# Attention and gated convolution in one kernel: the written order is planned anew, with a new model of the DMA queue

## The chip, the cores and the metric

The kernel runs on one core of a Trainium2 chip. The metric is the device time of one execution in microseconds (us), lower is better. Before the change it is 386.22 us (median of 3 runs, 385.4 to 386.39).

## What is computed

For each of 8 batches and 12 heads, with 448 rows and 64 columns a head, in float32:

```python
scores = q @ k.T / 8
m = scores.max(-1)
e = exp(scores - m)
attn = e / (e.sum(-1) + exp(-m) + 1e-9)       # softmax with one more in the sum
x = attn @ v                                   # heads side by side: 448 x 768 a batch
x1, x2, x3 = split(x @ w_proj, 3)              # w_proj is 768 x 2304
c = irfft(rfft(x2, axis=rows) * rfft(filter))  # circular convolution along the 448 rows
out = (x1 * c * x3) @ w_out
```

## The kernel before, in words

Matmuls run in bfloat16. Two heads form a pair: six pairs a batch, 48 in all, numbered 0 to 47. For pair i the kernel has these steps, named by the tokens that they make in the code:

- Loads of q, k and v (192 or 224 KB each), cast to bfloat16 by GpSimd (POOL). For the first two batches (`staged`, pairs 0 to 11) TensorE (PE) transposes q and k, step `T`. For the others (`loaded`) a DMA does it, a "turn" (`k_turn`, `q_turn`, tokens `kT` and `qT`): one pair each for batch 2, three pairs each from batch 3 on.
- `S(i,0..3)`: four groups of scores on PE (lines 772 and 774). ScalarE (ACT) takes the exponential of each (lines 785 and 791). `ER` and `V(i,0..1)`: the products with v (lines 803 and 811). `norm` on VectorE (DVE, lines 824 to 826) divides and leaves `xb`.
- `X`: xb transposed into xT, by PE in batch 0 and by a DMA of three pairs (`x_dma`, line 896) after that.

Then, a batch b at a time, the dense part (`dense`):

- `fold` and `xf` on DVE (lines 954 to 962): sums and differences of xT, two halves of three pairs.
- `P(b,pg,ch)`: eight groups of six matmuls for x2 (line 985). `Z`: 8 matmuls into the spectrum (line 1012), copied by ACT (`xs`, line 1020), multiplied and added by DVE (`t` and `yh`, lines 1026 and 1032).
- `I(b,0..5)`: the way back (line 1097), copied by ACT (line 1106), put together by DVE (`cw`, `cv`, `y`, lines 1115 to 1141).
- `G(b,0..5,0..1)`: twelve groups of six for x1 and x3 (line 1058), drained by ACT (line 1070) and DVE (line 1073).
- `O`: the groups for the output (line 1170), drained by ACT (line 1182) and stored.

The filter's spectrum (`hps`, lines 724 and 727, 16 matmuls) is made once. The weights come in pieces through POOL's queue, cast on the way: `LOADS` names them, (1,0) and (1,1) the two halves for P, (0) and (2) for G, "F" the filter, "O" w_out (`wout`, line 755).

No engine chooses its order at run time. `Plan` holds all steps as tasks, each with an engine, a cost, a due time ("want"), the tokens that it needs and makes, and for a DMA the time that it takes on the transfer engines. `Plan.run` walks through planned time, and when an engine is free it takes the first task within a window of 160 that is ready, in order of due times. The outcome is one fixed sequence of instructions for each engine; semaphores hold them to the data. So a wrong cost makes no wrong result, but it may put an instruction too early in a queue, and all that stands behind it on that queue waits with it. SyncE's queue (SP) issues all loads, turns and stores in such a sequence. The due times come from tables: `ATT` and `SLOT` (attention), `DENSE` and `PACE` (dense part), `FOLD`, `LEAD` (how long before its pair a load, cast or turn is due), `LOAD` (weights). In the first 36 us of planned time gaps on PE are filled with matmuls of zeros (line 1256), behind 38 at the start (line 1264).

Planned costs before the change, and one of the lines that hold them:

```python
    LANDING = 2.2
    LEAD = [4.72, 83.18, 8.95, -3.90, 7.63, -20.62, 94.14]
    add("SP", 1.3, tau(g) - LEAD[6], lambda hp=hp: q_turn(hp), need=[("cq", i) for i in gs] + [last],
        make=[("qT", i) for i in gs], dma=0.5 * few, late=0.7)
```

Of the kernel before, what the change touches and what calls it, by code (L numbers as in the profile page):

```python
# [20 lines left out]
SP = 112  # L21
# [20 lines left out]
class Plan:  # L42
# [10 lines left out]
    LAT = {"PE": 0.2, "ACT": 0.22, "DVE": 0.2, "POOL": 0.15, "SP": 0.0}  # L53
    LANDING = 2.2
    OPEN = 8
# [12 lines left out]

    def add(self, eng, cost, want, emit, need=(), make=(), take=(), give=(), dma=0.0, run=256, n=1, after=0.0, begun=(), late=0.0):
        self.tasks.append((want, len(self.tasks), eng, cost, emit, need, make, take, give, dma, after, run, n, begun, late))  # L70

    def run(self):
# [13 lines left out]
        gone = {}  # L86
        free = {e: self.BEGIN for e in queue}
        now, order = 0.0, []
        events = [0.0] + sorted({t[10] for t in self.tasks})
        queues = {"SP": [], "POOL": []}  # L90
# [166 lines left out]
def kernel(  # L257
# [124 lines left out]
    def staged(b):  # L382
# [3 lines left out]
        for hp in range(NHP):  # L386
# [5 lines left out]
            for n, (name, x, at, size) in enumerate(parts):  # L392
                src = stage(g, at, size)

                def load(name=name, x=x, src=src, hp=hp, g=g):
# [12 lines left out]
                first = name == "q" and g == 0  # L408
                add("ACT" if first else "SP", 0.52, -21.0 if first else want + 0.1 * n, load, need=need,
                    make=[("s" + name, g)], dma=0.75 if name == "q" else 0.7 if g or name == "v" else 1.5, run=1024 if name == "q" else 768,  # L410
                    begun=[("i" + name, g)])
                if hp == 0 and name != "q":
                    add("SP", 0.5, want + (0.05 if name == "k" else SLOT[0] + 0.05) if b == 0 else want - RE1 + 0.1 * n,
                        lambda name=name, x=x: nc.sync.dma_start(rests[:, "kv".index(name)], shared(x, b)),
                        need=[("cr" + name, b - 1)] if b else (), make=[("r" + name, b)],
                        dma=1.05, begun=[("ir", b)])

# [107 lines left out]
    def loaded(b):  # L525

        i0 = b * NHP
        few = 1 if b == NSTAGED else 3
# [17 lines left out]
        for n, (name, x) in enumerate((("k", k), ("v", v))):  # L546
            add("SP", 0.5, tau(i0) - LEAD[0] - 0.2 + 0.1 * n,
                lambda name=name, x=x: nc.sync.dma_start(rests[:, "kv".index(name)], shared(x, b)),
                need=[("cr" + name, b - 1)], make=[("r" + name, b)], dma=1.05)
        for u in range(2):  # L550
            c = slice(64 * u, 64 * u + 64)
            add("POOL", 0.6, tau(i0) - LEAD[1] - 0.2, lambda c=c: nc.gpsimd.tensor_copy(kn[c, :, 0, c], rests[c, 0]),
                need=[("rk", b)] + (["zero kn"] if b == NSTAGED else [("kT", i) for i in range(i0 - NHP, i0)]), make=[("crk", b)])
        add("POOL", 0.56, tau(i0) - LEAD[3], lambda: nc.gpsimd.tensor_copy(vn[b % 2][:, :, 3, 0:DH], rests[:, 1]),
            need=[("rv", b), ("V", i0 - NHP - 1, 1)], make=[("crv", b), ("vr", b)])

        for hp in range(NHP):
            g = i0 + hp
            n = g - NHP * NSTAGED
            qsrc = qrooms[n % QS]  # L560
            add("SP", 0.52, tau(g) - LEAD[4],
                lambda hp=hp, qsrc=qsrc: nc.sync.dma_start(
                    qsrc.rearrange("p (u c) -> p u c", u=2),
                    q[b, 2 * hp : 2 * hp + 2].rearrange("u (p j) d -> p u (j d)", j=NST),
                ),
                need=[("cq", g - QS)] if n >= QS else staged_done, make=[("sq", g)], dma=0.75, run=1024)
            add("POOL", 0.65, tau(g) - LEAD[5],
                lambda hp=hp, qsrc=qsrc: nc.gpsimd.tensor_copy(  # L568
# [4 lines left out]
            if hp % few == 0:  # L573
                gs = range(g, g + few)
                add("SP", 1.3, tau(g) - LEAD[6], lambda hp=hp: q_turn(hp), need=[("cq", i) for i in gs] + [last],
                    make=[("qT", i) for i in gs], dma=0.5 * few, late=0.7)
            for n, (name, x) in enumerate((("k", k), ("v", v))):
# [4 lines left out]
                    ("T", i) for i in range(NHP * NSTAGED - NHP, NHP * NSTAGED)]  # L582
                add("SP", 0.52, tau(g) - LEAD[0] + 0.1 * n,
                    lambda x=x, hp=hp, src=src: nc.sync.dma_start(src.rearrange("p (u c) -> p u c", u=2), rows(x, b, hp)),
                    need=room, make=[("s" + name, g)], dma=0.7, run=768)
                sv = src.rearrange("p (u j d) -> p u j d", u=2, j=3)
                if name == "k":
                    add("POOL", 0.6, tau(g) - LEAD[1],
                        lambda hp=hp, sv=sv: nc.gpsimd.tensor_copy(
# [170 lines left out]
    def attention(i):  # L760
# [168 lines left out]
    def dense(b):  # L929
# [264 lines left out]
        def O(st, ch):  # L1194
# [42 lines left out]
    with (  # L1237
# [102 lines left out]
```

## Time and profile before

| what | value |
|---|---|
| median of 3 runs | 386.22 us |
| span of the profiled execution | 384.4 us |
| what lies around the span: median less span | 1.8 us |
| PE busy | 364.9 us, 95% |
| PE loading weights | 232.4 us, 60% |
| DVE busy | 261.8 us, 68% |
| ACT busy | 264.1 us, 69% |
| POOL busy | 112.2 us, 29% |
| DMA packets, bytes | 116333, 64.43 MB |

The profile is of one execution. Its time as a run is not given beside it, so its own time is its span and 1.8 us around it, as the median has it. PE's busy time counts the matmuls of zeros too. A wait is put down to what ended it last. The share of DMA is the mean over 16 DMA engines, and it can pass 1 where packets overlap.

### The profile page before, as it was taken

Reading aid. Unit: us, or ns where it says so; the run is one execution under the profiler, and the core shown is the slowest. Engines: PE = TensorE matmul, PEld = TensorE weight load, DVE = VectorE, ACT = ScalarE, POOL = GpSimd, SP = SyncE. Lnnn points to the kernel's source line nnn. Section 1 sums busy time; section 2 is a strip of 40 time slices with the busy share of each in tenths; the row PEclk is TensorE's granted clock in tenths of the full one; section 3 lists DMA queues with packets and bytes.
Section 4 is the critical chain, followed back from the end, with each engine's and each line's share of the span. In section 5 each row is a group of like instructions: output and inputs, shape, how many; then the busy total and the mean of one; then the engine's idle time right before and its main releaser. Section 6 shows DMA issues by size and latency. Waiting matters only on the chain.

```text
span 384.4 us, 9536 instructions
## 1 busy us (share of the span) xinstructions
PE 364.9 (95%) x3700; PEld 232.4 (60%) x3700; DVE 261.8 (68%) x667; ACT 264.1 (69%) x460; POOL 112.2 (29%) x240
## 2 busy tenths in 40 slices
PE   7887799999998999889989999999999999999995
PEld 6555575557654676545755666565665567667553
DVE  6575758996868357997596576665488725987660
ACT  5698487884885868767756658886778587444543
POOL 5692436141835533445552411110000000000000
PEclk9999999999999999999999999999999999999999
DMA  8999998599999999999999933592302132200214
GB/s 207 265 225 232 249 219 197 131 178 218 262 269 273 249 261 244 263 230 251 247 241 226 274 112 100 102 210 96 84 3 43 41 124 43 43 1 2 82 41 165
DMA packets 116333, 64.43 MB, mean 168 GB/s; under 512 B 73085, under 2 KB 112704, under 8 KB 116288
## 3 DMA queue, kind: packets, MB, share of 16 engines
q1 hardware_dynamic: 111568, 58.18, 63.5%
q0 software_dynamic: 4480, 5.41, 8.3%
q8 instruction: 29, 0.48, 0.5%
q10 hardware_dynamic: 240, 0.23, 0.3%
q14 instruction: 16, 0.13, 0.1%
HBM read 43.86 MB, written 11.01 MB: 143 GB/s over the span
## 4 chain that ended last, share of the span: by engine, by line
PE 65%; DVE 13%; DMA 12%; ACT 4%; issue 2%; POOL 2%; SPq 2%; POOLq 0%; DVEq 0%; ACTq 0%
PE psum L1058 19%; PE psum L985 14%; PE psum L1170 12%; PE psum L811 6%; PE psum L772 5%; DMA nat<-in_k_dram 5%; DMA xT<-xb 3%; DVE t L1026 2%; DMA nat<-in_v_dram 2%; PE psum L1097 2%; PE psum L1012 2%; DMA nat<-in_q_dram 2%; DVE xf L962 2%; DVE yh L1032 2%; ACT e L785 2%
## 5 line engine op out<-in xcount | busy, mean ns | idle before, releaser
L785 ACT ACTIVATE e<-psum 128x896 bf16<-128x896 f32 x144 | 126.4, 925 | 21.8 <-PE psum L772 21.6
L1058 PE MATMUL psum<-xT,wproj_bf 128*128 128x448 bf16 x576 | 122.4, 352 | 0.1
L1058 PEld LDWEIGHTS <-wproj_bf 128*128 128x128 bf16 x576 | 53.5, 97 | 42.8 <-issue 1.3
L985 PE MATMUL psum<-wproj_bf,xf 128*113 128x384 bf16 x384 | 69.1, 326 | 1.5 <-DVE g L1073 0.7
L985 PEld LDWEIGHTS <-xf 128*113 128x113 bf16 x384 | 50.0, 132 | 15.3 <-issue 3.4
L1170 PE MATMUL psum<-wout_bf,yT 128*128 128x384 bf16 x288 | 52.9, 326 | 0.0
L811 PE MATMUL psum<-vn,e 128*128 128x65 bf16 x1152 | 44.7, 194 | 0.0
L1070 ACT CAST x<-psum 128x448 bf16<-128x448 f32 x48 | 25.6, 534 | 25.8 <-PE psum L1058 24.5
L1026 DVE TENSOR_TENSOR t<-xs,hrs 113x768 bf16<-113x768 bf16 (+1 forms) x64 | 37.0, 613 | 8.0 <-ACT xs L1020 8.0
L772 PE MATMUL psum<-qT,kT 64*128 64x448 bf16 x288 | 40.8, 355 | 0.6 <-ACT kT L485 0.4
L1182 ACT COPY osb<-psum 128x384 f32<-128x384 f32 x56 | 26.4, 484 | 21.3 <-PE psum L1170 20.0
L811 PEld LDWEIGHTS <-e 128*128 128x128 bf16 x1152 | 39.2, 97 | 2.8
L568 POOL CAST nat<-nat 112x512 bf16<-112x512 f32 x36 | 24.1, 671 | 52.6 <-DMA nat<-in_q_dram 49.2
L1170 PEld LDWEIGHTS <-yT 128*128 128x128 bf16 x288 | 27.5, 98 | 19.2 <-issue 1.5
L824 DVE TENSOR_SCALAR rec<-psum 128x8 f32<-128x8 f32 x48 | 7.7, 161 | 44.8 <-PE psum L811 44.3
L1073 DVE TENSOR_TENSOR g<-x,psum 128x448 bf16<-128x448 bf16 x48 | 29.5, 615 | 11.9 <-PE psum L1058 9.5
L999 ACT CAST x<-psum 113x384 bf16<-113x384 f32 x32 | 15.5, 483 | 28.7 <-PE psum L985 28.5
L826 DVE TENSOR_TENSOR xb<-psum,rec 128x512 bf16<-128x512 f32 x48 | 33.2, 691 | 1.7
L1020 ACT CAST xs<-psum 113x384 bf16<-113x384 f32 (+1 forms) x64 | 28.2, 499 | 3.8 <-PE psum L1012 3.6
L1106 ACT CAST cr<-psum 128x452 bf16<-128x452 f32 x48 | 25.3, 547 | 7.0 <-PE psum L1097 6.6
L791 ACT ACTIVATE er<-psum 128x448 bf16<-128x448 f32 x48 | 26.7, 556 | 4.6 <-PE psum L774 4.6
L997 DVE CAST x<-psum 113x384 bf16<-113x384 f32 x32 | 17.5, 550 | 14.1 <-PE psum L985 14.1
(111 smaller groups left out, 435.7 us busy)
## 6 DMA issues: line engine op xcount, KB each, us to landing
nat<-in_q_dram SPq DMA_DIRECT2D x47, 224.0 KB, 4.7
out_dram<-osb SPq DMA_DIRECT2D x24, 384.0 KB, 2.4
nat<-in_k_dram SPq DMA_DIRECT2D x41, 192.0 KB, 4.9
nat<-in_v_dram SPq DMA_DIRECT2D x41, 192.0 KB, 4.9
wproj_bf<-in_moe_w_proj_dram POOLq DMA_DIRECT2D x2, 1152.0 KB, 17.3
rests<-in_k_dram SPq DMA_DIRECT2D x8, 192.0 KB, 4.9
rests<-in_v_dram SPq DMA_DIRECT2D x8, 192.0 KB, 5.2
out_dram<-osb SPq DMA_DIRECT2D x8, 192.0 KB, 2.9
```

The costliest lines, as they stand in the source:

```text
L772: nc.tensor.matmul(sc[:, u, 0:S], kT[b % 2][c, hp, t, :], qT[b % 2][c, hp, :])
L785: nc.scalar.activation(to, of, AF.Exp, scale=SCALE)
L791: nc.scalar.activation(to, of, AF.Exp, scale=SCALE)
L811: nc.tensor.matmul(out_bank(u)[:, n, :], P["e"][1 + t][:, u * S + n * 128 : u * S + n * 128 + 128], vn[b % 2][:, hp, 4 * u + t, :], start= ...
L826: nc.vector.tensor_tensor(W["xb", b][:, hp].rearrange("p n (u d) -> p u n d", u=2), op[:, :, :, 0:DH], rec[:].unsqueeze(3).to_broadcast([1 ...
L985: nc.tensor.matmul(pps[:FQ, :DCH], W["xf", b][:, pg, kt, 0:FQ], wproj_bf[:, kt, D + ch * DCH : D + (ch + 1) * DCH], start=(kt == 0), stop= ...
L1020: nc.scalar.copy(L["xs", par, ch][:K, pg % 2, :], L["Z", pg, ch][:K, :DCH])
L1026: nc.vector.tensor_tensor(t[:K], L["xs", par, ch][:K], h, op=ALU.mult)
L1058: nc.tensor.matmul(p[:, :S], wproj_bf[:, kt, 2 * part * D + dt * 128 : 2 * part * D + (dt + 1) * 128], xT()[:, kt, 0:S], start=(kt == 0), ...
L1073: nc.vector.tensor_tensor(g[:, dt, :], L["x1", dt], p[:, :S], op=ALU.mult)
L1170: nc.tensor.matmul(ops[:n, :DCH], y[:, dt, 0:n], wout_bf[:, dt, ch * DCH : (ch + 1) * DCH], start=(dt == 0), stop=(dt == NDT - 1),)
L1182: nc.scalar.copy(L["os", st][:n, ch * DCH : (ch + 1) * DCH], L["O", st, ch][:n, :DCH])
```

## The change

It changes no computation and no instruction: every engine has the same instructions (but for the matmuls of zeros, 76 at line 1256's place in the code where there were 97). It changes what the planner believes, and so the order and the places of the instructions on every queue.

- A DMA that transposes (`turn=True`) now holds the planned SP queue: SP is free again 0.7 before the transfer ends or 0.86 after the issue began, whichever is later. Before, SP was free after 1.3.
- The planned duration of each transfer is new, as is the landing (1.95 for 2.2), and an issue costs SP 0.3 for 0.5.
- `LEAD` is a table per batch, where one row served all.
- All due times are new. Among what follows from them: through POOL's queue the weights go as F, (1,0), (0), (1,1), (2), O, where it was (1,1), (0), F, (1,0), (2), O; w_out is issued behind the casts of pair 13, where it was behind those of pair 16; the filter's spectrum stands ahead of the first P; O of batch 0 and of batch 2 stand soon after their I, where they stood 17 and 36 us of PE work behind.

```diff
-    LANDING = 2.2
+    LANDING = 1.95
+    TURN_ISSUE, TURN_LEAD = 0.86, 0.7
+    SHIFT = {}
...
+                        if h[2][15]:
+                            free[e] = max(clock - self.TURN_LEAD, begin[h[2][1]] + self.TURN_ISSUE)
+                            heapq.heappush(events, free[e])
                         done(h[2], clock + self.LANDING + h[2][14], "SP")
...
-                    q.append([end, t[9], t])
+                    if t[15]:
+
+                        begin[t[1]], free[e] = now, 1e9
+                    q.append([now + 0.3 if t[15] else end, t[9], t])
...
-    EARLY1 = -5.85
-    ATT = [-63.37, 36.20, 83.38, 128.18, 122.21, 218.64, 210.09, 292.26]
-    SLOT = [1.36, 6.40, 8.21, 8.91, 11.38, 2.68, 4.29, 4.12]
-    DENSE = [50.42, 77.73, 144.20, 160.20, 213.12, 281.73, 315.75, 367.72]
-    PACE = [2.71, 3.56, 3.39, 2.66, 1.44, 0.79, 2.71, 1.39]
-    FOLD = [3.84, -32.37, -15.20, -28.40, -33.99, 9.69, -1.20, -1.70]
-    BPS = -25.34
-    RE1 = 46.00
-    WT = -31.32
-    FT = 0.83
-    LEAD = [4.72, 83.18, 8.95, -3.90, 7.63, -20.62, 94.14]
+    EARLY1 = -5.43
+    ATT = [-48.42, 1.92, 93.57, 111.14, 46.91, 245.01, 205.42, 222.14]
+    SLOT = [0.14, 5.03, 9.86, 14.97, 9.04, 0.61, -10.27, -1.1]
+    DENSE = [72.83, 96.28, 173.19, 181.62, 199.31, 235.42, 279.1, 331.47]
+    PACE = [2.15, 3.1, 1.53, 2.94, 3.31, 0.92, 2.69, 1.81]
+    FOLD = [-20.68, -115.55, -25.95, -41.02, -47.18, 42.45, -7.31, -135.3]
+    BPS = -24.09
+    RE1 = -2.37
+    WT = -75.21
+    FT = 2.66
+    LEAD = [[-29.25, -101.67, 38.04, 55.9, 5.24, -130.87, 20.71], [-25.94, 112.17, -40.27, 4.11, 13.86, 16.28, 149.16], [41.81, 129.15, -260.24, -85.45, -172.23, -121.12, 99.32], [-164.22, 158.39, -19.35, -139.68, -71.05, -159.36, 143.98], [-83.86, -75.27, 82.11, -52.7, 29.14, -263.4, 8.34], [56.73, 232.93, 64.7, 148.75, -29.25, 49.97, 136.56]]
     LOADS = ((1, 0), (1, 1), ("F", None), (0, None), (2, None), ("O", None))
-    LOAD = [36.80, 17.95, 27.44, 19.56, 37.20, 81.70]
+    LOAD = [11.77, 23.74, -18.08, 13.81, 41.73, 65.45]
...
-    FOLD0 = [58.39, 87.97, 7.09]
+    FOLD0 = [42.14, 22.78, -69.07]
...
+        lead = LEAD[b - NSTAGED]
...
-                add("SP", 1.3, tau(g) - LEAD[6], lambda hp=hp: q_turn(hp), need=[("cq", i) for i in gs] + [last],
-                    make=[("qT", i) for i in gs], dma=0.5 * few, late=0.7)
+                add("SP", 1.3, tau(g) - lead[6], lambda hp=hp: q_turn(hp), need=[("cq", i) for i in gs] + [last],
+                    make=[("qT", i) for i in gs], dma=(0.55, 0.91)[few > 1], run=860, late=0.2, turn=True)
...
-                        add("SP", 1.3, tau(g) - LEAD[2], lambda hp=hp: k_turn(hp), need=[("ck", i) for i in gs] + [("crk", b), last],
-                            make=[("kT", i) for i in gs], dma=0.6 * few, late=0.7)
+                        add("SP", 1.3, tau(g) - lead[2], lambda hp=hp: k_turn(hp), need=[("ck", i) for i in gs] + [("crk", b), last],
+                            make=[("kT", i) for i in gs], dma=(1.06, 1.77)[few > 1], run=860, late=0.2, turn=True)
...
-                    make=[m for h in ps for m in (("X", NHP * b + h), ("xT", b, h))], dma=0.5 * len(ps), late=1.2)
+                    make=[m for h in ps for m in (("X", NHP * b + h), ("xT", b, h))], dma=(0.0, 0.89, 1.26, 1.48)[len(ps)], run=860, late=0.2, turn=True)
...
-                add("POOL", 0.95, at, wout_load, make=["wout"], dma=6.9, run=1500, after=at)
+                add("POOL", 0.95, at, wout_load, make=["wout"], dma=6.04, run=1900, late=1.5, after=at)
```

More of the change, by code (lines that the diff above doesn't have):

```diff
@@ L67, in __init__, with add @@
         self.banks = {}
-    def add(self, eng, cost, want, emit, need=(), make=(), take=(), give=(), dma=0.0, run=256, n=1, after=0.0, begun=(), late=0.0):
-        self.tasks.append((want, len(self.tasks), eng, cost, emit, need, make, take, give, dma, after, run, n, begun, late))
+    def add(self, eng, cost, want, emit, need=(), make=(), take=(), give=(), dma=0.0, run=256, n=1, after=0.0, begun=(), late=0.0, turn=False, part=None):
+        want += self.SHIFT.get(part, 0.0)
+        self.tasks.append((want, len(self.tasks), eng, cost, emit, need, make, take, give, dma, after, run, n, begun, late, turn))
     def run(self):
@@ L87, in run @@
         free = {e: self.BEGIN for e in queue}
+        begin = {}
         now, order = 0.0, []
-        events = [0.0] + sorted({t[10] for t in self.tasks})
+        events = sorted({0.0, self.BEGIN, *(t[10] for t in self.tasks)})
         queues = {"SP": [], "POOL": []}
@@ L408, in staged @@
                 first = name == "q" and g == 0
-                add("ACT" if first else "SP", 0.52, -21.0 if first else want + 0.1 * n, load, need=need,
-                    make=[("s" + name, g)], dma=0.75 if name == "q" else 0.7 if g or name == "v" else 1.5, run=1024 if name == "q" else 768,
+                add("ACT" if first else "SP", 0.52 if first else 0.3, -21.0 if first else want + 0.1 * n, load, need=need,
+                    make=[("s" + name, g)], dma=0.78 if name == "q" else 0.66 if g or name == "v" else 1.3, run=860,
                     begun=[("i" + name, g)])
                 if hp == 0 and name != "q":
-                    add("SP", 0.5, want + (0.05 if name == "k" else SLOT[0] + 0.05) if b == 0 else want - RE1 + 0.1 * n,
+                    add("SP", 0.3, want + (0.05 if name == "k" else SLOT[0] + 0.05) if b == 0 else want - RE1 + 0.1 * n,
                         lambda name=name, x=x: nc.sync.dma_start(rests[:, "kv".index(name)], shared(x, b)),
                         need=[("cr" + name, b - 1)] if b else (), make=[("r" + name, b)],
-                        dma=1.05, begun=[("ir", b)])
+                        dma=1.43, run=860, begun=[("ir", b)])
                 on_pool = g > 0
@@ L546, in loaded @@
         for n, (name, x) in enumerate((("k", k), ("v", v))):
-            add("SP", 0.5, tau(i0) - LEAD[0] - 0.2 + 0.1 * n,
+            add("SP", 0.3, tau(i0) - lead[0] - 0.2 + 0.1 * n,
                 lambda name=name, x=x: nc.sync.dma_start(rests[:, "kv".index(name)], shared(x, b)),
-                need=[("cr" + name, b - 1)], make=[("r" + name, b)], dma=1.05)
+                need=[("cr" + name, b - 1)], make=[("r" + name, b)], dma=1.5, run=860)
         for u in range(2):
             c = slice(64 * u, 64 * u + 64)
-            add("POOL", 0.6, tau(i0) - LEAD[1] - 0.2, lambda c=c: nc.gpsimd.tensor_copy(kn[c, :, 0, c], rests[c, 0]),
+            add("POOL", 0.6, tau(i0) - lead[1] - 0.2, lambda c=c: nc.gpsimd.tensor_copy(kn[c, :, 0, c], rests[c, 0]),
                 need=[("rk", b)] + (["zero kn"] if b == NSTAGED else [("kT", i) for i in range(i0 - NHP, i0)]), make=[("crk", b)])
-        add("POOL", 0.56, tau(i0) - LEAD[3], lambda: nc.gpsimd.tensor_copy(vn[b % 2][:, :, 3, 0:DH], rests[:, 1]),
+        add("POOL", 0.56, tau(i0) - lead[3], lambda: nc.gpsimd.tensor_copy(vn[b % 2][:, :, 3, 0:DH], rests[:, 1]),
             need=[("rv", b), ("V", i0 - NHP - 1, 1)], make=[("crv", b), ("vr", b)])
@@ L560, in loaded @@
             qsrc = qrooms[n % QS]
-            add("SP", 0.52, tau(g) - LEAD[4],
+            add("SP", 0.3, tau(g) - lead[4],
                 lambda hp=hp, qsrc=qsrc: nc.sync.dma_start(
@@ L565, in loaded @@
                 ),
-                need=[("cq", g - QS)] if n >= QS else staged_done, make=[("sq", g)], dma=0.75, run=1024)
-            add("POOL", 0.65, tau(g) - LEAD[5],
+                need=[("cq", g - QS)] if n >= QS else staged_done, make=[("sq", g)], dma=0.87, run=860)
+            add("POOL", 0.65, tau(g) - lead[5],
                 lambda hp=hp, qsrc=qsrc: nc.gpsimd.tensor_copy(
@@ L582, in loaded @@
                     ("T", i) for i in range(NHP * NSTAGED - NHP, NHP * NSTAGED)]
-                add("SP", 0.52, tau(g) - LEAD[0] + 0.1 * n,
+                add("SP", 0.3, tau(g) - lead[0] + 0.1 * n,
                     lambda x=x, hp=hp, src=src: nc.sync.dma_start(src.rearrange("p (u c) -> p u c", u=2), rows(x, b, hp)),
-                    need=room, make=[("s" + name, g)], dma=0.7, run=768)
+                    need=room, make=[("s" + name, g)], dma=0.75, run=860)
                 sv = src.rearrange("p (u j d) -> p u j d", u=2, j=3)
                 if name == "k":
-                    add("POOL", 0.6, tau(g) - LEAD[1],
+                    add("POOL", 0.6, tau(g) - lead[1],
                         lambda hp=hp, sv=sv: nc.gpsimd.tensor_copy(
@@ L601, in cast @@
                             nc.gpsimd.tensor_copy(vn[b % 2][:, hp, 4 * u : 4 * u + 3, 0:DH], sv[:, u])
-                    add("POOL", 0.72, tau(g) - LEAD[3], cast, need=[("sv", g), ("V", g - 2 * NHP, 1)], make=[("cv", g), ("v", g)])
+                    add("POOL", 0.72, tau(g) - lead[3], cast, need=[("sv", g), ("V", g - 2 * NHP, 1)], make=[("cv", g), ("v", g)])
     tab = {}
@@ L1210, in O @@
             if ch == 1:
-                add("SP", 0.6, w, lambda: store(st), need=[("os", b, st)], make=[("store", b, st)], give=[os_], dma=1.4, run=3072)
+                add("SP", 0.3, w, lambda: store(st), need=[("os", b, st)], make=[("store", b, st)], give=[os_], dma=0.87 if st < 3 or b % 2 else 0.45, run=2600)
         if b:
@@ L1294 @@
             if part == "F":
-                add("POOL", 1.6, at, filter_load, need=["ft", "bps"], make=["filt"], take=[("yT", "F")], dma=4.1, run=1500, n=3, after=at)
+                add("POOL", 1.6, at, filter_load, need=["ft", "bps"], make=["filt"], take=[("yT", "F")], dma=4.84, run=1900, n=3, late=1.5, after=at)
             elif part == "O":
-                add("POOL", 0.95, at, wout_load, make=["wout"], dma=6.9, run=1500, after=at)
+                add("POOL", 0.95, at, wout_load, make=["wout"], dma=6.04, run=1900, late=1.5, after=at)
             elif ch is None:
-                add("POOL", 0.95, at, lambda part=part: wproj_load(part, None), make=[("w", part, 0), ("w", part, 1)], dma=6.9,
-                    run=1500, after=at)
+                add("POOL", 0.95, at, lambda part=part: wproj_load(part, None), make=[("w", part, 0), ("w", part, 1)], dma=6.04,
+                    run=1900, late=1.5, after=at)
             else:
-                add("POOL", 0.7, at, lambda part=part, ch=ch: wproj_load(part, ch), make=[("w", part, ch)], dma=3.5, run=1500, after=at)
+                add("POOL", 0.7, at, lambda part=part, ch=ch: wproj_load(part, ch), make=[("w", part, ch)], dma=3.02, run=1900, late=1.5, after=at)
         more_tables()
```

## The prediction, made before the changed kernel was run

> **What bounds the kernel now.** I read the page's engine totals first, then busy time by stretches, then PE's waits, then the queues around the places where PE waited.
>
> ```profile
> PE 364.9 (95%) x3700; PEld 232.4 (60%) x3700; DVE 261.8 (68%) x667; ACT 264.1 (69%) x460; POOL 112.2 (29%) x240
> ```
>
> PE is the bound. Same instructions give the same PE work, so the change can move only PE's idle time and the zeros. Where that time lies (columns: stretch, its length, then busy time of PE, PEld, DVE, ACT, POOL, then clock, DMA share, GB/s):
>
> ```profile
> 0.00:46.20 46.20, 36.89 (x574) 27.29 (x575) 29.17 (x89) 33.05 (x47) 27.23 (x71) 1.00 1.08 236
> 46.20:58.20 12.00, 11.88 (x110) 8.76 (x107) 7.14 (x15) 8.88 (x19) 3.73 (x7) 1.00 1.10 218
> 58.20:117.30 59.10, 58.58 (x589) 35.76 (x588) 48.65 (x117) 43.92 (x78) 26.56 (x50) 1.00 0.98 209
> 117.30:156.00 38.70, 37.26 (x389) 23.44 (x387) 24.46 (x59) 28.54 (x50) 18.26 (x38) 1.00 1.13 257
> 156.00:200.00 44.00, 39.95 (x411) 24.41 (x408) 36.46 (x83) 30.28 (x51) 22.22 (x44) 1.00 1.07 252
> 200.00:380.60 180.60, 180.33 (x1647) 112.77 (x1644) 115.93 (x308) 118.94 (x218) 14.23 (x32) 1.00 0.37 93
> 380.60:384.50 3.90, 0.00 (x0) 0.00 (x0) 0.00 (x0) 0.44 (x1) 0.00 (x0) 0.77 0.55 180
> ```
>
> PE idles 9.3 us in the head (and runs zeros in more of it), 1.4 and 4.05 in two stretches, hardly at all after 200 us, and 3.9 in the tail. DMA is full up to 200 us. Who ended the waits (us, times, longest):
>
> ```profile
> PE psum L466 <- POOL k L424: 3.3, 4, 1.6
> PE psum L1097 <- DVE g L1073: 2.9, 3, 1.2
> PE psum L774 <- DMA qT<-nat: 1.1, 1, 1.1
> PE psum L985 <- DVE g L1073: 0.7, 1, 0.7
> ```
>
> These are: transposes of staged pairs waiting for k (head); VectorE late in 156 to 200; and one late q turn, S(18) at 119.69.
>
> To compare orders I lay PE's work end to end at the trace's start-to-start spacings: six matmuls at L1058 1.14, six at L985 or L1170 0.98, 24 at L811 0.76, four at L772 0.48 (0.1 more behind another shape), eight at L803 0.12, one at L774 0.19, four at L1097 0.21, a `T` 0.43. It sums to 352.9 us, the zeros at the start included, in both orders. The work ahead of a step is its mark; start less mark is the delay. Before, the delay is 13.7 at V(5), 16.5 at the first P, 18.6 at mark 34, 19.4 at S(12), 21.2 at S(18), 22.8 at I(2,0), 26.6 at I(3,0), 27.5 at the end. 352.9 + 27.5 + 4.0 of tail give the span.
>
> **The change part by part.** *Planner costs and fillers.* They issue nothing: 0. The 21 fewer zeros (56 ns each, 1.2 us) stood in gaps; the clock row is 1.00 throughout. The order of the last steps is the same: tail 0.
>
> *Head.* V(5) has mark 20.6 in both, behind the same six pairs: 0, though k of pair 4 now loads ahead of v of pair 3 (the longest early wait, 1.5, may shrink), and 1.15 us of POOL memsets leave an idle place for one among casts. V(5) to the first P took 5.8 us (34.8 to 40.6: norm, transposes, copy, fold); the new order has 3.6 of work in it (now `hps`, 16 matmuls), so the delay becomes 13.8 + 2.2 = 16.0. `hps` needs the filter: its first piece stands at the same place in POOL's queue as the first weight did (issue 20.51), with nothing ahead; that weight landed after 9.4, so the filter lands near 31, plus 1.8 of DVE adds, against 34.8. Then `T(9)`, which waited 1.76 for k, has mark 32.0 instead of 26.7, so starts at 48.0 against a cast at 44.48: gone. `T(11)` (42.8, so 58.8) is covered by 1.6 us against its cast at 56.65. The three ACT-drained steps put earlier (`hps` 3.0 us, four of x2 1.9) fill ACT's gap there, 33 of 46 us. Delay 16.0 where it was 18.6: -2.6 (0 to -4.1, since loads and weights are the same bytes at a full DMA, and the 1.5 may go).
>
> *First turned pairs and w_out.* SP now issues the x turn of pairs 6 to 8 ahead of the turns of pairs 12 and 13. It waits for V(8) (mark 42.2, so 58.2) and 1.05 of norm; 1.56 of issue; four turns at 1.2 to 2.6 end near 66.5 and land 2.4 to 4.8 later, 69 to 71.3. S(12) has mark 57.0 (54.3 before), 73 to 74; S(13) three later. Covered by 2.5. But w_out is now in flight there. Before, it was issued at 82.12, and these two k turns went beside it:
>
> ```profile
> 82.12 0.82 POOL L755 DMA_DIRECT2D wout_bf<-in_moe_w_out_dram  x1
> ...
> 82.50 2.77 SPq L540 DMA_TRANSPOSE kT<-nat  x2
> ...
> DMA to landing us min/median/max: 8.7/9.2/9.7
> ```
>
> The three at 68.32 without it:
>
> ```profile
> 68.32 4.45 SPq L540 DMA_TRANSPOSE kT<-nat  x3
> ...
> DMA to landing us min/median/max: 2.4/2.4/2.6
> ```
>
> I take +0.7, nearer to the turns alone since only a part overlaps (0 to +3.5). The Trainium skill, "DMA: Bandwidth & Descriptors", section "Queues, rings and completion order", says that each DMA engine takes turns between the queue rows packet by packet; the 9.2 against 2.4 agrees. By that rule every turn in w_out's 10.9 us is slowed and the sum below would be 2.8 higher; by the row of turns alone, 0.7 lower.
>
> *Later turns.* S(18)'s wait goes, -1.3 with its restart (bound 0): x turn ready at mark 88, then x 2.4, q 2.4, 0.4, and k landing 4.7 after issue end at 98.0; S(18) has 101.0. Next late are S(21), whose k turn stands behind two stores (ready at 109.3, landing 6.1 later, 115.4 against 118.7), and S(24), behind store(1,3) (139.7 against 141.9). SP's order allows both by 2 to 3 us, but it waited up to 4.4 us on landings before: +1.2 (0 to +4).
>
> *VectorE.* In 156 to 200, DVE did the fold of the next batch inside the chain that frees I:
>
> ```profile
> 162.74 0.69 DVE L1117 TENSOR_TENSOR cw<-cr 128x444 bf16<-128x444 bf16 x1
> ...
> 166.20 1.83 DVE L1117 TENSOR_TENSOR cw<-cr 128x444 bf16<-128x444 bf16 x1
> ```
>
> By row means, DVE's queue from t to the last yh of batch 2 held 8.1 us (two folds, four xf in it) and from cw to y of batch 3 12.2 us (folds, two norms). In the new order these are 5.2 and 5.0, without folds. Batch 3's t to yh keeps a fold (6.1 us in 6.8 of PE work), and batch 4's room from its last Z to I shrinks from 6.45 to 3.80. So of the 4.9 us of waits at I(2), I(2,5), P(3), V(28) and I(3) I keep 2.3: -2.6 (-4.9 to +8, see below).
>
> Sum: -2.6 + 0.7 - 1.3 + 1.2 - 2.6 = -4.6. Against the profiled execution (384.4 and 1.8 around it, which is the median) that is 381.6 us.
>
> **The rivals.** *The DMA system gives it back.* DMA's share is 0.98 to 1.13 up to 200 us, so a PE that comes earlier finds turns late. Price: w_out holds the four turns by 6.3, so S(12) and S(13) wait 3.5, and SP stays behind, so that S(21) and S(24) cost 4: -4.6 + 2.8 + 2.8 = +1.0, 387.2, or about 386 if one of the two comes. For it: the 9.2 row. Against: in the head PE reaches these marks no earlier than the last staged load.
>
> *DVE in lumps* (the slower end). DVE work that becomes ready per 20 us of PE work is 20.6, 21.3 and 20.3 at marks 80, 120 and 200 in the new order, over PE's 20 each time; before, past mark 60, at most 18.7. If each lump costs what 156 to 200 cost (4.05 idle), 12.2 take the place of 4.05: -2.6 + 0.7 - 1.3 + 1.2 + 8.1 = +6.1, 392.3. It decides from 2.0 us a lump. Against: each lump is followed by 8 to 13 us windows, and the chains to I are free of folds.
>
> **How the numbers follow.** Forecast 0.60, own range 379 to 384. DMA 0.18, spread evenly over the three outcomes. DVE lumps 0.22, slower. The forecast gives 0.57 faster and 0.03 same (0.3%, 1.2 us, is about what a measurement can tell from no change). So faster 0.63, same 0.09, slower 0.28. For 8 in 10 the range leaves out the ends of both: 377.5 (head and DVE at their better bounds) to 390 (two of three lumps).
>
> **What would show it.** PE idle up to 46 us below 9; no wait of `T(9)`; S(12), S(18), S(21), S(24) without a wait on a turn; under 2.5 idle in the windows of batches 2 and 3; nothing new past 200 us. Wrong if PE waits on kT or qT near 73, or on DVE near 100, 140 or 225.

## The result, and the profile after

The changed kernel takes 389.45 us (median of 20 runs, 387.55 to 398.77) beside 386.31 us for the kernel before (20 runs, 384.68 to 390.99): ratio 1.0087, 95% interval 1.0068 to 1.0107. It is slower by 0.9% where 1.2% faster was forecast. Measured once more beside the last experiments it had the same ratio, 1.0087 (1.0047 to 1.0127). The medians are of all runs, while the ratios leave out those in which the chip was in a slower state, and the two differ by up to 0.4%.

The engine totals of the changed kernel's page:

```profile
PE 366.3 (95%) x3679; PEld 233.0 (60%) x3679; DVE 263.1 (68%) x667; ACT 265.1 (69%) x460; POOL 114.7 (30%) x240
```

The instructions are the same (but for 21 fewer zeros), yet PE is counted busy for 1.4 us more, and its idle time gives only 0.4 of the 1.8 us between the two spans. Why is open; the delays below go by starts and hold both parts. Busy time by stretches of the changed kernel, the columns as before:

```profile
0.00:46.20 46.20, 40.38 (x543) 30.26 (x544) 30.35 (x88) 36.24 (x58) 28.13 (x73) 1.00 1.10 243
46.20:58.20 12.00, 11.77 (x141) 8.20 (x140) 10.34 (x24) 9.06 (x17) 4.95 (x9) 1.00 1.14 228
58.20:117.30 59.10, 55.86 (x548) 33.36 (x545) 43.89 (x106) 39.93 (x70) 21.28 (x41) 1.00 0.93 199
117.30:156.00 38.70, 37.82 (x382) 23.50 (x378) 25.32 (x65) 28.80 (x49) 15.81 (x35) 1.00 1.05 236
156.00:200.00 44.00, 41.65 (x422) 25.75 (x422) 32.23 (x75) 31.18 (x55) 22.02 (x42) 1.00 1.05 237
200.00:382.50 182.50, 178.78 (x1655) 111.97 (x1654) 120.98 (x314) 119.56 (x216) 22.54 (x43) 1.00 0.41 101
382.50:386.20 3.70, 0.00 (x0) 0.00 (x0) 0.00 (x0) 0.34 (x1) 0.00 (x0) 0.90 0.52 178
```

PE idles 5.8 us in the head (9.3 before), 3.2 from 58 to 117 (0.5), 2.35 from 156 to 200 (4.05) and 3.7 past 200 (0.3). The head gained, and the rest took as much back (0.4 us of idle time more in all). What ended PE's waits:

```profile
PE psum L916 <- DVE xb L837: 2.7, 3, 1.5
PE psum L1181 <- DVE g L1084: 2.3, 2, 1.9
PE psum L785 <- DMA qT<-nat: 1.7, 1, 1.7
PE psum L1069 <- DVE xb L837: 1.4, 2, 0.8
PE psum L1108 <- DVE xb L837: 1.0, 1, 1.0
...
PE psum L814 <- DVE g L1084: 1.0, 1, 1.0
```

L916 is the head. L785 is S(12) at 75 us. The others shown are O, G, I and V, and all wait for VectorE: a releaser `xb` or `g` is often just the last operation of VectorE's backlog, which frees the PSUM bank. (Lines of the changed kernel stand 10 or 11 further down: L837 is `norm`, L1084 `g`, L1126 to L1152 `cw`, `cv`, `y`, L1037 and L1043 `t` and `yh`.)

Delay (start less mark, as in the prediction) at seven marks, for one profiled execution each:

| kernel | 40 | 60 | 100 | 140 | 180 | 240 | end |
|---|---|---|---|---|---|---|---|
| before | 18.6 | 19.4 | 21.2 | 22.8 | 26.6 | 27.1 | 27.5 |
| changed | 14.4 | 18.1 | 19.7 | 21.1 | 26.1 | 27.5 | 29.2 |
| changed, again (e13) | 15.1 | 18.6 | 21.6 | 22.2 | 27.8 | 29.3 | 31.0 |
| e1: its head, then the old order | 14.8 | 17.4 | 21.8 | 26.7 | 29.7 | 30.4 | 30.8 |
| e2: the old head, then its order | 18.4 | 21.1 | 23.6 | 24.1 | 28.7 | 30.1 | 32.5 |
| e4: no load of w_out | 15.2 | 17.3 | 20.0 | 20.2 | 26.9 | 28.6 | 30.3 |
| e5: short casts | 15.2 | 18.4 | 19.5 | 20.1 | 21.1 | 22.1 | 25.3 |
| e6: short casts, kernel before | 19.7 | 19.8 | 23.0 | 23.4 | 26.3 | 26.7 | 27.1 |
| e14: three moves, again | 14.3 | 18.2 | 21.1 | 22.6 | 26.4 | 30.2 | 30.7 |
| e15: short casts, no w_out | 15.7 | 18.8 | 19.6 | 19.6 | 21.1 | 21.2 | 23.0 |

A wait is named by the step whose start it delays; it can lie inside the step ahead (for V(28) in its `ER`, L814; for O(2,0,0) in e7 and e8 in the group of scores ahead of it). The two profiled executions of the changed kernel differ by up to 1.9 us at a mark, so single waits are read from the profiles and verdicts from the times. The kernel before had medians of 386.98 us beside e1 to e4, 388.45 beside e5 to e8, 388.08 beside e9 to e12 and 387.43 beside e13 to e15; each ratio goes by the runs beside it.

### The profile page after: what moved, and what is told of

Its sections match the earlier page's. It is cut to its first block, busy times and chain, and to the rows that moved or that the text cites. A ratio compares the mean times of both kernels' runs of the same rounds, so it can differ in the third digit from the quotient of the medians.

```text
span 386.2 us, 9454 instructions
## 1 busy us (share of the span) xinstructions
PE 366.3 (95%) x3679; PEld 233.0 (60%) x3679; DVE 263.1 (68%) x667; ACT 265.1 (69%) x460; POOL 114.7 (30%) x240
## 4 chain that ended last, share of the span: by engine, by line
PE 70%; DVE 18%; DMA 4%; issue 2%; ACT 2%; SPq 2%; POOL 0%; ACTq 0%; POOLq 0%; DVEq 0%
PE psum L1069 20%; PE psum L996 15%; PE psum L1181 10%; PE psum L822 7%; PE psum L783 6%; DVE t L1037 4%; DMA qT<-nat 2%; DVE yh L1043 2%; PE psum L785 2%; DVE xb L837 2%; PE psum L1108 2%; PE psum L1023 2%; DVE g L1084 2%; SPq L551 2%; DVE xf L973 1%
## 5 line engine op out<-in xcount | busy, mean ns | idle before, releaser
L796 ACT ACTIVATE e<-psum 128x896 bf16<-128x896 f32 x144 | 126.7, 921 | 25.9 <-PE psum L783 25.3
L1181 PE MATMUL psum<-wout_bf,yT 128*128 128x384 bf16 x288 | 51.6, 326 | 2.4 <-DVE g L1084 2.3
L1081 ACT CAST x<-psum 128x448 bf16<-128x448 f32 x48 | 25.7, 536 | 27.6 <-PE psum L1069 22.8
L579 POOL CAST nat<-nat 112x512 bf16<-112x512 f32 x36 | 24.9, 695 | 58.8 <-DMA nat<-in_q_dram 58.5
L1037 DVE TENSOR_TENSOR t<-xs,hrs 113x768 bf16<-113x768 bf16 (+1 forms) x64 | 38.0, 628 | 6.1 <-ACT xs L1031 6.1
L1181 PEld LDWEIGHTS <-yT 128*128 128x128 bf16 x288 | 27.2, 98 | 22.2 <-issue 4.7
L1193 ACT COPY osb<-psum 128x384 f32<-128x384 f32 x56 | 26.1, 483 | 17.1 <-PE psum L1181 15.5
L837 DVE TENSOR_TENSOR xb<-psum,rec 128x512 bf16<-128x512 f32 x48 | 33.2, 691 | 1.7
L1084 DVE TENSOR_TENSOR g<-x,psum 128x448 bf16<-128x448 bf16 x48 | 29.4, 615 | 6.2 <-PE psum L1069 5.9
L1010 ACT CAST x<-psum 113x384 bf16<-113x384 f32 x32 | 15.4, 486 | 24.1 <-PE psum L996 23.8
L612 POOL CAST vn<-nat 128x192 bf16<-128x192 f32 x58 | 23.0, 425 | 22.6 <-DMA nat<-in_v_dram 12.6
```

Of the source, the lines that this page charges most:

```text
L796: nc.scalar.activation(to, of, AF.Exp, scale=SCALE)
L837: nc.vector.tensor_tensor(W["xb", b][:, hp].rearrange("p n (u d) -> p u n d", u=2), op[:, :, :, 0:DH], rec[:].unsqueeze(3).to_broadcast([1 ...
L1037: nc.vector.tensor_tensor(t[:K], L["xs", par, ch][:K], h, op=ALU.mult)
L1081: nc.scalar.copy(L["x1", dt], p[:, :S])
L1084: nc.vector.tensor_tensor(g[:, dt, :], L["x1", dt], p[:, :S], op=ALU.mult)
L1181: nc.tensor.matmul(ops[:n, :DCH], y[:, dt, 0:n], wout_bf[:, dt, ch * DCH : (ch + 1) * DCH], start=(dt == 0), stop=(dt == NDT - 1),)
```

## The experiments

**Where the head's gain goes (e1 to e3).** The order is written out as task numbers, and the planner is held to it. For e1 and e2 one kernel's plan is followed up to mark 41, then the other's; for e3 the changed one up to mark 209.

```diff
-    WINDOW = 160
+    WINDOW = 1
+    ORDER = {"PE": "7 28 425 29 ...", "ACT": ...}
...
-        queue = {e: sorted(t for t in self.tasks if t[2] == e) for e in self.LAT}
+        queue = {e: [self.tasks[int(i)] for i in self.ORDER[e].split()] for e in self.LAT}
```

> The plan of the changed kernel up to S(9,2) (mark 41, the end of the head), and from there the order of the kernel before on every engine. At that point PE stood 14.4 us behind its marks in the changed kernel and 18.6 in the kernel before. Theory 'each order has its own waits': the changed kernel lost its head gain to waits that its later order made, so with the old order behind it the 4.2 us stay: end delay 23.3 instead of 27.5, 382.1 us, 0.989 of the kernel before. Rival 'the loads set the pace': a PE that comes 4 us early finds the turns of pairs 12 to 24 and the casts late, waits on qT and kT grow by 4 us by S(24), and the time is that of the kernel before, 386 us, 1.00. In between: 384, with 2 us of waits on turns.

Measured: 388.12 us, 1.0041 (1.0009 to 1.0072). The head gained its 4 us (14.8 at mark 40) and lost them by mark 70, first at S(14), which waited 2.65 us for its q turn; the seam then cost more (P(2,0,1) 1.7, S(21) 0.9, I(2,0) 1.7). The gain was not kept, as the rival had it. How much of the loss belongs to the place where the two plans meet was not separated.

> The reverse: the order of the kernel before up to Z(0,2,0) (mark 41), and from there the plan of the changed kernel. Theory 'each order has its own waits': the head's 4.2 us are lost and the later waits stay, 393.6 us, 1.019 of the kernel before. Rival 'the loads set the pace': a PE that comes 4 us later finds the turns landed, the wait of S(12) (1.9 us) and those around w_out go, and the time is that of the changed kernel, 389.5, 1.008.

Measured: 390.24 us, 1.0069 (1.0037 to 1.0101), not to be told from the changed kernel. By the times the head's 4 us are worth nothing that can be measured, as the rival said: the 1.019 of the theory lies outside the interval. Its one profile says less, since it ends 1.5 and 3.3 us behind the two of the changed kernel. And the rival's mechanism did not show: S(12) waited 2.14 us here too, with a PE that came later. So that wait is not a matter of a PE that is early. The four turns stand on SP behind the x turn of pairs 6 to 8, which waits for PE's own V(8), so they move along with PE.

> The plan of the changed kernel up to V(31,0) behind the last Z of batch 4 (mark 209, delay 26.2), from there the order of the kernel before. Theory 'each order has its own waits': the waits of the changed kernel on VectorE behind that point (I(4,0) 1.2, G(5,0,1) 0.6, P(5,0) 0.4, some small ones) go and the 0.5 us of the order before come, so the end delay is 26.7 where the changed kernel had 29.2: 2.5 us under the changed kernel, 386.9 us, 1.002 of the kernel before. Rival 'VectorE is behind by then, whatever comes next': the same work waits in another place, and the time stays within 0.8 us of the changed kernel, 1.007.

Measured: 397.75 us, 1.0242 (1.0181 to 1.0302). The two orders do not fit at this seam: S(36,1) waited 2.2 and V(35) 3.5 for VectorE, where neither kernel has such a wait. It tells nothing on the question.

**w_out beside the turns (e4).**

```diff
-        nc.gpsimd.dma_start(wout_bf, moe_w_out.rearrange("(t p) c -> p t c", p=128))
+        nc.gpsimd.memset(wout_bf, 0.01)
```

> The changed kernel with the load of w_out left out: a memset to 0.01 on GpSimd stands in its place, so the last product is taken with a constant matrix. Orders and all other work are those of the changed kernel. Theory 'w_out slows the turns beside it': the four turns of pairs 12 and 13 land some 2.4 us after issue instead of 7.0 to 10.2, S(12) waits 0 instead of 1.9 us, and the delay at mark 62 is 16 instead of 18.1; if what comes later keeps it, 387.4 us, 1.003. Rival 'the turns are late since the x turn of pairs 6 to 8 stands ahead of them on the same queue': S(12) still waits 1.5 us or more, and the time is that of the changed kernel.

The two k turns of pairs 12 and 13, issue and landing, from 62 to 73 us of the changed kernel:

```profile
wout_bf<-in_moe_w_out_dram POOLq DMA_DIRECT2D x1, 1152.0 KB, 11.8
...
kT<-nat SPq DMA_TRANSPOSE x2, 10.0
```

and without the load of w_out:

```profile
kT<-nat SPq DMA_TRANSPOSE x2, 4.0
```

The q turns behind them landed after 2.4 us instead of 7.0 and 8.8, and S(12) did not wait. 387.67 us, 1.0014 (0.9978 to 1.0049): 0.7% under the changed kernel. But the delay at mark 60 was 17.3, where 16 had been expected, and O4(2,0,0) waited 3.2 us instead of 2.0, so that in the profile part of what was won was lost to VectorE later.

**The casts (e5, e6).** What VectorE did ahead of O4(2,0,0) in the changed kernel (start, duration):

```profile
165.52 0.75 DVE L1126 TENSOR_TENSOR cw<-cr 128x452 bf16<-128x452 bf16 x1
166.19 1.70 DVE L1128 TENSOR_TENSOR cw<-cr 128x444 bf16<-128x444 bf16 x1
167.92 1.33 DVE L1137 TENSOR_TENSOR cv<-cw 128x448 bf16<-128x448 bf16 x2
169.18 0.61 DVE L1084 TENSOR_TENSOR g<-x,psum 128x448 bf16<-128x448 bf16 x1
```

GpSimd at the same time:

```profile
165.06 0.96 POOL L600 CAST nat<-nat 128x384 bf16<-128x384 f32 x2
165.96 0.77 POOL L579 CAST nat<-nat 112x512 bf16<-112x512 f32 x1
166.68 0.50 POOL L600 CAST nat<-nat 128x384 bf16<-128x384 f32 x1
167.14 0.51 POOL L600 CAST nat<-ks 128x384 bf16<-128x384 f32 x1
167.59 0.66 POOL L600 CAST nat<-nat 128x384 bf16<-128x384 f32 x1
168.20 0.77 POOL L579 CAST nat<-nat 112x512 bf16<-112x512 f32 x1
```

and PE:

```profile
169.84 1.46 PE L1181 MATMUL psum<-wout_bf,yT 128*128 128x384 bf16 x8 [1.89 <-DVE g L1084]
```

The second `cw` took 1.70 us, and 0.39 with no cast beside it; the two `cv` 1.33, and 0.69. The 1.95 us more are the 1.89 that PE waited. It is not this place alone. The operations of the changed kernel, sorted by whether a cast of GpSimd ran beside them (worked out from the trace; median and longest in ns):

| operation, inputs | no cast: count, median | cast beside: count, median, longest |
|---|---|---|
| `t` L1037, both in SBUF | 34, 551 | 30, 692, 1306 |
| `yh` L1043, both in SBUF | 39, 351 | 25, 493, 764 |
| `cv` L1137, both in SBUF | 37, 387 | 11, 526, 851 |
| `cw` L1128, both in SBUF | 21, 387 | 3, 386, 1703 |
| `g` L1084, one in PSUM | 32, 615 | 16, 610, 622 |
| `xb` L837, one in PSUM | 23, 691 | 25, 691, 692 |

The time of all operations over the median of their form with no cast beside, the stretch, is 18.5 us in the kernel before and 19.6 in the changed one. Past 156 us it is 8.7 (6.6 up to 200 us, 1.6 up to 260, 0.5 behind) and 10.8 (5.7, 4.5, 0.6): the changed order has more of it in 200 to 260 us, where three of its waits behind VectorE are. In that window GpSimd is busy for 22.2 us in the changed kernel and for 14.2 in the one before: the new order has moved casts into it. The Trainium skill, "SBUF — State Buffer", section "Summary: rules for kernel authors", says that when a VectorE instruction has two inputs in SBUF while a GpSimd instruction reads SBUF, the second one to issue is blocked until the first finishes. The table agrees on which forms are hit. On the length it differs: the `cw` of 1.70 lasted past three casts of 0.5 to 0.8 us, not one.

The test cuts the casts of batches 3 to 7, the same five edits for q, k, v and the last rows, in both kernels:

```diff
+        wd = 8 if b > NSTAGED else DH
...
-                            kn[:, hp, 1:4].rearrange("p j (u d) -> p u j d", u=2), sv
+                            kn[:, hp, 1:4].rearrange("p j (u d) -> p u j d", u=2)[:, :, :, 0:wd], sv[:, :, :, 0:wd]
```

> The changed kernel with GpSimd's casts of batches 3 to 7 cut to 8 of 64 columns of each head (the other columns keep the values of an earlier batch, so the output is not the reference's). Orders and all other instructions are those of the changed kernel. Theory 'casts stretch VectorE': in the changed kernel VectorE's operations from SBUF to SBUF last 10.2 us longer between 156 and 260 us than the same forms do with no cast beside them; with short casts this falls under 3 us, and the waits behind VectorE (O4(2,0,0) 2.0, V(28) 1.2, G(3,3,0) 0.9, I(4,0) 1.2; 5.3 in all) fall by 4 or more: 385 us, 0.997 of the kernel before. Rival 'VectorE has too much queued in those places, stretched or not': the four waits keep 4 us or more, and the time is 388 or above, 1.005.

> The same cut of GpSimd's casts in the kernel before. Theory 'casts stretch VectorE': the 4.05 us that PE idles between 156 and 200 us fall to 1.5 or less, 383.5 us, 0.993; the changed kernel then stays behind by what its other waits cost (S(12), G(5,0,1), P(5,0)). Rival 'VectorE has too much queued': 3 us or more of the 4.05 stay, 386, 1.00.

The same place with short casts, VectorE:

```profile
163.73 0.39 DVE L1127 TENSOR_TENSOR cw<-cr 128x452 bf16<-128x452 bf16 x1
164.04 0.38 DVE L1129 TENSOR_TENSOR cw<-cr 128x444 bf16<-128x444 bf16 x1
164.46 0.69 DVE L1138 TENSOR_TENSOR cv<-cw 128x448 bf16<-128x448 bf16 x2
165.10 0.62 DVE L1085 TENSOR_TENSOR g<-x,psum 128x448 bf16<-128x448 bf16 x1
```

and PE behind it, with no wait:

```profile
166.49 1.46 PE L1182 MATMUL psum<-wout_bf,yT 128*128 128x384 bf16 x8
```

In e5 the stretch from 156 to 260 us is 0.5 us instead of 10.2. O4(2,0,0), G(3,3,0) and I(4,0) no longer wait, V(28) 0.5: 4.8 of 5.3 us are gone. 383.68 us, 0.9856 (0.9800 to 0.9912), 2.3% under the changed kernel, more than was expected. A short cast also ends sooner, so turns behind it may start earlier. By the delays that is the lesser part at most: at mark 140 e5 is 1.0 us ahead of the first profile of the changed kernel and 2.1 ahead of the second, at mark 240 5.4 and 7.2, and the waits that went between these marks are those behind VectorE. Past mark 240 it loses 1.5 again: G(5,0,1) waited 2.0 for its x turn (0.6 in the changed kernel). G(4,0,1), at mark 197, waited 0.9 for one where there was no such wait.

In e6 the waits at I(2), P(3) and V(28) went and 0.4 is left at I(3,0), but one of 2.0 behind VectorE's `xb` came ahead of G(3,0,1), so that about half of the 4.05 us stays (2.1), between the two expectations; S(14) and S(18) waited 1.7 and 1.4 for q turns: 386.12 us, 0.9959 (0.9917 to 1.0000). So whole casts cost the kernel before 0.4%, hardly clear of nothing, and the changed one 2.3%. With the casts out of the way the changed order is the faster one: 0.9856 to 0.9959 is a ratio of 0.990 (worked out from the two intervals, some 0.983 to 0.997).

**Moves against single waits (e7 to e9, e14).** They change places in the written order alone, for instance in VectorE's list (numbers of the tasks; 1316 to 1319 are `cw` and `cv` of (2,2), 1325 is g(2,5)):

```diff
-1316 1317 1318 1319 1325
+1316 1325 1317 1318 1319
```

> The changed kernel with its order written out, and two moves on VectorE alone: the product g(2,5) goes ahead of the second cw of (2,2), and the six fold steps of batch 4's first three pairs go from the middle of batch 3's t and yh to behind batch 3's last y. Theory 'what PE waits for stands behind other work in VectorE's queue': O4(2,0,0) waits 0.3 or less instead of 2.0, V(28) and G(3,3,0) 0.3 or less together instead of 2.1, the rest stays: 385.5, 0.998 of the kernel before. Rival 'the waits only move on': the next steps that need VectorE (O(2,0,0), I(3,0), I(4,0)) wait 2 us or more longer than in the changed kernel, and the time is 388 or above.

Measured: 389.59 us, 0.9996 (0.9952 to 1.0040). By the ratios that is 0.9% under the changed kernel, which was measured in another session, and by the medians (388.45 for the kernel before, beside it) 0.5%. O4(2,0,0) did not wait, and O(2,0,0) behind it waited 1.9. V(28) and G(3,3,0) did not wait; S(28,3) 0.3 and G(4,0,1) 0.7 did.

> The kernel of the two VectorE moves, and two moves more: on PE O(3,2,1) and O(3,3,0) go ahead of S(32,3), so that 2 us of PE work stand between the last Z of batch 4 and I(4,0); on SP the x turn of pairs 33 to 35 goes ahead of the two kT turns of batch 7. Theory as there: I(4,0) no longer waits (1.2), G(5,0,1) and P(5,0,0) no longer wait for the late x turn (1.0 together); with the 4 us of the VectorE moves 383.3, 0.992, less than both kernels. Rival 'the waits only move on': the two O steps wait for their banks or batch 4's G steps wait later for lack of them, and the time is 386 or above.

In the changed kernel the x turn of pairs 33 to 35 stood on SP behind four turns of batch 7, which waited for the last S of batch 5:

```profile
256.14 3.61 SPq L544 DMA_TRANSPOSE qT<-nat  x2
259.84 3.65 SPq L551 DMA_TRANSPOSE kT<-nat  x2
263.59 1.76 SPq L907 DMA_TRANSPOSE xT<-xb  x1
```

Measured: 389.19 us, 1.0023 (0.9978 to 1.0067). I(4,0), G(5,0,1) and P(5,0,0) no longer waited; G(4,0,1) waited 2.0, O(2,0,0) 1.7, and three steps of batch 4 1.5 together.

> The changed kernel with its order written out and three moves: on VectorE only the second half of the fold of batch 4's first three pairs (w and two xf, 1.8 us) goes behind the y of (3,1); on PE only O(3,2,1) goes ahead of S(32,3); on SP the x turn of pairs 33 to 35 goes ahead of batch 7's kT turns. The move of g(2,5), which only passed its wait on to O(2,0,0), is left out. Theory 'what PE waits for stands behind other work in its queue': V(28) and G(3,3,0) wait 0.6 or less instead of 2.1, I(4,0) 0.3 or less instead of 1.2, G(5,0,1) and P(5,0,0) 0.2 or less instead of 1.0, and G(4,0,1), which waited 2.0 when the whole fold was moved, 0.5 or less: 386, 0.999 of the kernel before. Rival 'the waits only move on': 2 us or more of them come again by mark 260, 388.5, 1.006.

Measured: 387.87 us, 1.0011 (0.9968 to 1.0053). Its profile, in which S(12) alone waited 6.6 us, is not read; e14 repeats it.

> The changed kernel once more, beside the two runs below on one chip. If its loss does not depend on the chip and the hour: 1.0087 of the kernel before, 1.006 to 1.011. If what the later comparisons showed for other versions (0.9996 to 1.0023) was the kernel before running slower there: 1.002 or less.

> The three moves once more (half a fold behind y of (3,1) on VectorE, O(3,2,1) ahead of S(32,3) on PE, the x turn of pairs 33 to 35 ahead of batch 7's kT turns on SP), on the same chip as the changed kernel itself. Theory 'late waits stand behind other work in a queue': 2 to 3 us under the changed kernel in the same rounds, as 1.0011 against 1.0087 had it. Rival 'the moves did nothing and the reference had drifted': within 1 us of the changed kernel. Its first profile was taken in a disturbed execution (S(12) waited 6.6 us); this one should show V(28), I(4,0), G(5,0,1) without their waits (2.9 us together).

Measured on one chip: the changed kernel 389.68 us, 1.0087 (1.0047 to 1.0127); the moves 388.99 us, 1.0060 (1.0026 to 1.0093). In the two profiles the moves took 3.9 us of waits away (V(28) and G(3,3,0) 2.1 to 0.5, I(4,0) 1.25 and G(5,0,1) with P(5,0,0) 1.0 to 0), and 3.4 came in other places: V(29) 1.4, G(4,2,1) 1.4, V(33) 0.5. Most of the waits moved on. The two measurements put the moves 0.3% (beside the changed kernel itself, within the intervals) and 0.8% below it, and neither below the kernel before.

**Casts of v on ScalarE (e10 to e12).**

```diff
-                            nc.gpsimd.tensor_copy(vn[b % 2][:, hp, 4 * u : 4 * u + 3, 0:DH], sv[:, u])
+                            (nc.scalar.copy if b > NSTAGED else nc.gpsimd.tensor_copy)(vn[b % 2][:, hp, 4 * u : 4 * u + 3, 0:DH], sv[:, u])
...
-                    add("POOL", 0.72, tau(g) - lead[3], cast,
+                    add("ACT" if b > NSTAGED else "POOL", 0.72, tau(g) - lead[3], cast,
```

> The changed kernel with its order written out, and the casts of v of batches 3 to 7 (30 pairs, 39% of GpSimd's cast time there) on ScalarE at the same places of the plan; output and all else as in the changed kernel. Theory 'casts stretch VectorE': the stretch of 10.2 us between 156 and 260 us falls to about 6, the four waits behind VectorE from 5.3 to about 3; ScalarE gets about 20 us more in 120 us of idle time: 387.3, 1.002 of the kernel before. Rival 'ScalarE pays': its exponentials come late, PE waits 2 us or more for e before V, and the time is 390 or above, 1.010.

> The order of the kernel before, written out, with the same casts of v on ScalarE. Theory 'casts stretch VectorE': the 4.05 us that PE idles between 156 and 200 us fall by some 1.5, 384.8, 0.996. Rival 'ScalarE pays': PE waits 2 us or more for e, 388, 1.005. With the casts cut short this order gained only 0.4%, since the turns of later pairs held PE instead: 1.5 us is the most that is to be had.

> The three moves and the casts of v on ScalarE together, in the changed kernel. If both theories hold: 386 less 2 is 384, 0.994, under both kernels. Rival 'ScalarE pays' or 'the waits move on': 388 or above.

Measured: 391.82 us, 1.0090 (1.0053 to 1.0127); 390.15 us, 1.0034 (1.0004 to 1.0065); 393.53 us, 1.0128 (1.0079 to 1.0178). In e10 the stretch from 156 to 260 us fell from 10.2 to 7.9 us only, O4(2,0,0) still waited 1.9, and G(3,1,0) 1.3 and G(5,0,1) 2.1. PE did not wait for exponentials past 117 us. So the rival had the time and not its mechanism: 60 casts fewer on GpSimd (two for each of 30 pairs) took away only 2.3 us of the stretch. Why e10 gained nothing on the changed kernel (1.0087), and why e11 and e12 take longer than the same orders with all casts on GpSimd, was not shown. No version that does all the work came clearly under the kernel before (the lowest is e7, 0.9996).

**Both causes out (e15).**

> The changed kernel with both left out: GpSimd's casts of batches 3 to 7 cut to 8 of 64 columns, and the load of w_out replaced by a memset, so the output is not the reference's. Alone they gave 0.9856 (casts) and 1.0014 (w_out) where the changed kernel had 1.0087: 2.3% and 0.7% less. If the two causes lie one behind the other they add up: 0.978, 378.5 us. If what w_out costs is taken back at the x turns that follow, whatever the casts do: that of the casts alone, 0.985, 382 us. A head gain of 4 us that is kept would show as a delay under 17 at mark 140.

PE's longest waits:

```profile
PE psum L917 <- DVE xb L838: 2.4, 3, 1.1
PE psum L1070 <- DVE xb L838: 2.0, 1, 2.0
PE psum L483 <- POOL q L440: 1.3, 3, 0.5
PE psum L786 <- DMA kT<-nat: 1.2, 1, 1.2
```

381.03 us, 0.9841 (0.9794 to 0.9889), 8.65 us under the changed kernel on the same chip. L1070 is G(0,2,0) at 64 us, among the casts of batch 2, which were left whole (`yh` there took 2.92 us for two in e5, 0.70 alone). Against e5 the load of w_out adds 0.15%, within the intervals: the two causes mostly cover the same time, as the second expectation had it (0.978 lies outside the interval), and the casts carry the loss. The delay at mark 140 is 19.6 and not under 17, but 3.2 us ahead of the kernel before, where it was 2.9 ahead at mark 40: what the head gained is not lost on the way here.

## Why the prediction was wrong, by its own steps

By the delays, the changed kernel ends 1.7 us behind in the profiled executions (29.2 against 27.5): head -4.2 at mark 40, +2.9 from there to mark 60 (3.7 against 0.8), -0.4 to mark 140 (3.0 against 3.4), +3.4 from there to the end (8.1 against 4.7). The sum had -2.6, +0.7, -0.1 and -2.6. The medians differ by 3.1 us; the second profile of the changed kernel ends 3.5 behind, with -3.5, +2.7, +0.2 and +4.1 in the same stretches.

- *Head, -2.6:* right in mechanism, low in size. The filter landed at 29.0 (31 forecast), T(9) and T(11) did not wait, and the delay was 14.4 (15.1 in the second profile) where 16.0 was forecast: the better bound, -4.1.
- *First turned pairs and w_out, +0.7:* the wrong end of the range was taken. S(12) waited 1.9, and the turns took 7.0 to 10.2 us, as the row of 9.2 and the packet-by-packet rule had it, not 2.4. By the rule the sum was to be 2.8 higher, which makes this term +3.5; +2.9 was measured, though S(12) is only half of the 3.7; the rest is G(0,2,0) 0.8 and smaller waits behind VectorE, which the prediction did not have. The reason given, that only a part overlaps, was false: w_out was in flight from 62.1 to 73.9 us, and the four turns, issued from 63.0 to 68.4, landed from 73.2 to 75.4. Without the load (e4) the delay still grew by 2.1 us from mark 40 to 60, so w_out is worth some 1.5 of the 3.7.
- *Later turns, -1.3 + 1.2:* S(18) and S(21) did not wait, S(24) 0.4. The sum up to mark 140 came out near (-0.4), but by luck: other waits filled it, G(1,2,0) 0.75 and O of batch 1 1.4, behind VectorE, and the wait of the kernel before at I(2,0), 1.2, lies just ahead of mark 140. The 4.4 us from which the prediction took its +1.2 were two waits of SP together, the longest 3.2.
- *VectorE, -2.6: the step that failed,* by 6.0 us (+3.4 measured; 1.0 of that are S(24) and G(5,0,1), which wait for turns). Counted by single waits of PE on VectorE, 2.3 of 4.9 us were to be left, and past mark 140 there were 6.2. It counted VectorE's queue by row means, in which an operation costs the same anywhere, and it put the row of 1.83 us for a `cw` down to a chain with folds in it. That row was no fold: it is a `cw` of the form that takes 0.39 us alone, beside casts, which GpSimd ran from 165.88 to 168.40 us without a break. The chains to I were freed of folds, as the prediction said, and O4(2,0,0) directly behind one of them waited 2.0 us all the same, for a `cw` of 1.70. From 200 to 260 us the stretch is 4.5 us in the changed order, of which batch 4's `t` and `yh` have 2.2, and 1.6 in the old one, where they have none.
- *Rival "DMA system gives it back" (387.2):* its w_out part came (a term of +3.5, +2.9 measured), its S(21) and S(24) part did not.
- *Rival "DVE in lumps" (392.3):* right that VectorE decides and in the sign. Its lumps were to lie at marks 80, 120 and 200, by work that becomes ready; the waits behind VectorE were at 146, 176, 178 and 213, and e5 shows that they nearly all go when the casts do, with VectorE's work itself unchanged.
- *What would show it:* PE idle up to 46 us below 9 (5.8): met. T(9): met. S(12): not, and the sign of being wrong named for 73 us, PE waiting on a turn, came at 75. Under 2.5 idle for batch 3: 2.35 from 156 to 200 us, but only since the waits of V(28) and G(3,3,0) lie just past 200. Nothing new past 200 us: not, 3.7 us.
- *Ends of the wide range:* by the prediction's own terms they come to 377.8 and, with two lumps of 4.05, 388.3, not to 377.5 and 390.

With short casts the two orders stand at 0.990, close to the 0.988 that was forecast: the account without the stretch had the right sign, and the stretch turned it round. That the size is near too is in part luck. In the profiles e5 ends only 1.8 us ahead of e6, and not by the terms of the sum: 4.5 ahead at mark 40, 1.4 at 60, 4.6 at 240.

What stays open: why the casts of v on ScalarE (e10) take so little of the stretch away; and why the moves of e14 let new waits appear at just their number, beyond that VectorE stays behind while the casts run.

## What to carry to other kernels

Before summing an engine's queue by row means, look at the spread of one form: an operation that takes 0.39 us in 21 places and 1.7 in another has a cause that moves with the schedule, and a new order moves the operation into it or out of it. Where GpSimd casts and VectorE combines operands in SBUF, treat their overlap as a cost of its own, and sort a form's durations by what ran beside it. A move that takes one wait away may show little while the backlog that made it is still there (0.3% here, beside the changed kernel); take the cause out once, in a kernel that leaves that work out, to learn what the order is worth.

## What the runs showed of the hardware that was not expected

Operations of VectorE with both inputs in SBUF lasted up to 4.4 times as long beside casts of GpSimd (1703 ns against 387), and one of them was held past three casts in a row; operations with an input in PSUM kept their time within 1%. Cutting the casts to an eighth of the columns brought the stretch from 156 to 260 us from 10.2 to 0.5 us. With a transfer of 1152 KB issued from GpSimd in flight, the four turns beside it landed after 7.0 to 10.2 us, and after 2.4 to 4.4 without it.
